# Seven block products in place of eight for the output GEMM of four token blocks

## The chip, the cores and the metric

The kernel runs on one core of a Trainium2 chip. The metric is the device time of one execution in microseconds; before the change it is 1434.03 us, the median of three runs (1433.68 to 1438.57). The core's engines run their own instruction lists in order: TensorE (PE, with its weight loads as PEld), the vector engine (DVE), ScalarE (ACT), GpSimd (POOL), and SyncE (SP), which issues the DMAs.

## The reference

An attention step is followed by two gated MLPs ("MoE" in the names), all in float32:

```
scores = x @ state.T / 8 ; a = softmax ; xread = a @ state          # per batch and head
a2 = softmax(state @ x.T / 8) ; sread = a2 @ x
x  = concat(xread, sread)                    # 8 batches x (512 + 32) tokens, 512 wide
x  = ((x @ w_a) * (x @ w_b)) @ w_out         # first MoE, d_ff = 1536
out = (silu(x @ w_gate) * (x @ w_val)) @ w_out2   # second MoE, d_ff = 1536
```

The 8 batches are 8 blocks of 512 tokens; the 8 x 32 state tokens are one block of 256 more, the "s block".

## The kernel before

**Precision.** A float32 operand is kept as two parts, a high part that the matmul's fp32r format holds exactly and the remainder as a low part. A product takes three matmuls: high x high, high x low, low x high. Splitting is one cast on ACT and one subtraction on DVE (`hi_lo`, `split`). A *pass* here is one matmul of a 128 x 128 stationary tile with 512 moving columns. The weights come as 64-bit numbers and are converted on ACT, DVE and GpSimd (`convert`).

**First MoE.** d_ff is cut into 12 steps f of 128 columns; two steps make a step pair fp. The gate and value GEMMs of a step (`gemm`, line 670) multiply the attention weights (two tiles of 128 x 512, high and low) with products of state and w_a, w_b (`sw`, lines 457, 458, 474), 6 passes each. The gate's bank `ab0` is copied to SBUF, the value's bank `ab1` is multiplied into it on DVE (`moe`, line 689), and the result `a` is split into `hs`. The output GEMM (`out_part`, line 705) adds 4 x 3 passes per step into the four banks `po0` to `po3`, two steps behind. Blocks 0 to 3 go together in pieces of four steps, since the state products are being made then; after that come blocks 4, 5, 6, the s block and block 7, one after the other. The output weights `wo1` stay in SBUF.

**Second MoE.** Blocks go in pairs (u, v). For the gate and value GEMMs (`product`, line 798) a 2 x 2 block product is done with 7 products instead of 8, on sums of blocks and weights; so is its output GEMM: 2 x 2 over (u, v) and (even step, odd step) against the output columns in halves. `operand_sums` makes the sums of the hidden values on DVE, `unit` (line 957) is one of the 7 products for half of the columns over a *chunk* of 3 step pairs, 9 passes, and adds and stores the partial results (`acc`). The 14 units of a chunk are dealt out between the GEMMs of the next chunk (`between`). The second MoE's weights are made by `second_weights` from block 4 on, sent to DRAM (`w2`, `wt`) and loaded when wanted.

**Attention.** `attention` loads x, transposed, in four tiles, makes both score matrices and both softmaxes. For blocks 0 and 1 the scores by rows (`pr`, line 519) are matmuls of their own, 32 columns wide; for the others the transposed scores (`psc`, line 530) are turned on DVE.

**Order.** No engine's order is written by hand. `Program.order` simulates the engines with a cost per operation, and takes, of the tasks whose inputs are there, the one with the earliest due time `by`; the order in which it starts them is the instruction order. Tasks with `start` (loads, some splits) wait for the planner's clock, which TensorE's main work drives. `FIRST_US`, `STRETCH`, `LEAD`, `ATT`, `DUE`, `AHEAD_US` set due times and starts, `ROOM` and `RESERVE` the tiles in SBUF (42 "w" tiles of 4 KB per partition, 26 "h" tiles of 2 KB). Forty-four spare pairs of matmuls on an identity (`warm`, line 1069) fill places where TensorE would have nothing.

## Time and profile before

| | |
|---|---|
| median of 3 runs | 1434.03 us |
| the profiled execution's own time | 1437.74 us |
| its span, first to last instruction | 1436.0 us |
| busy: PE / PEld / DVE / ACT / POOL | 1427.4 / 1181.3 / 1010.6 / 712.3 / 105.2 us |
| mean granted TensorE clock | 0.995 of 2.4 GHz |
| DMA, all queues | 344.26 MB, 240 GB/s, 67.7% of 16 engines |

The busy time of an engine is the time in which it has at least one instruction running. Matmuls overlap: one lasts some 390 ns, and the next starts some 226 ns after it. So the price of a matmul is read from the distance of starts, or from how many fit in a stretch, and not from its duration. The same holds, less so, for DVE and ACT.

### The profile page before, as it was taken

Reading aid. Unit: us, or ns where it says so; the run is one execution under the profiler, and the core shown is the slowest. Engines: PE = TensorE matmul, PEld = TensorE weight load, DVE = VectorE, ACT = ScalarE, POOL = GpSimd, SP = SyncE. Lnnn points to the kernel's source line nnn. Section 1 sums busy time; section 2 is a strip of 40 time slices with the busy share of each in tenths; the row PEclk is TensorE's granted clock in tenths of the full one; section 3 lists DMA queues with packets and bytes.
Section 4 is the critical chain, followed back from the end, with each engine's and each line's share of the span. In section 5 each row is a group of like instructions: output and inputs, shape, how many; then the busy total and the mean of one; then the engine's idle time right before and its main releaser. Section 6 shows DMA issues by size and latency. Waiting matters only on the chain.

```text
span 1436.0 us, 20514 instructions
## 1 busy us (share of the span) xinstructions
PE 1427.4 (99%) x7344; PEld 1181.3 (82%) x7344; DVE 1010.6 (70%) x1722; ACT 712.3 (50%) x1264; POOL 105.2 (7%) x78
## 2 busy tenths in 40 slices
PE   9999999999999999999999999999999999999998
PEld 7777788778787878998888888888888888888887
DVE  6799857875778787875796895556855477554454
ACT  6677756753556566644654453335333353323340
POOL 3102201100011101111010000000000000000000
PEclk9999999999999999999999999999999999999999
DMA  8874853943456757856988795766947578376476
GB/s 292 277 255 166 282 201 126 313 166 113 154 215 247 260 209 261 309 201 220 380 317 289 266 381 205 261 227 213 371 149 263 183 278 294 132 251 223 144 260 237
DMA packets 134424, 344.26 MB, mean 240 GB/s; under 512 B 14001, under 2 KB 16049, under 8 KB 134321
## 3 DMA queue, kind: packets, MB, share of 16 engines
q1 hardware_dynamic: 134320, 342.94, 67.7%
q8 instruction: 58, 0.95, 0.3%
q14 instruction: 46, 0.37, 0.1%
HBM read 246.42 MB, written 95.94 MB: 238 GB/s over the span
## 4 chain that ended last, share of the span: by engine, by line
PE 95%; DVE 2%; ACT 1%; DMA 1%; SPq 0%; issue 0%; ACTq 0%; DVEq 0%
PE pX L798 18%; PE p L670 17%; PE po L705 17%; PE pu L957 16%; PE pC L798 9%; PE pY L798 5%; PE p_s L670 2%; PE po_s L705 1%; PE pvs L670 1%; PE pgs L670 1%; PE sw L457 1%; PE pus L1012 1%; PE sw L458 1%; DMA xt<-in_xt 1%; PE psc L530 1%; PE pr L519 1%
## 5 line engine op out<-in xcount | busy, mean ns | idle before, releaser
L705 PE MATMUL po<-hs,wo 128*128 128x512 f32 x1152 | 283.3, 391 | 0.1
L705 PEld LDWEIGHTS po<-hs,wo 128*128 128x128 f32 x1152 | 214.7, 188 | 47.1 <-issue 1.6
L957 PE MATMUL pu<-S,wt 128*128 128x512 f32 x1008 | 242.7, 389 | 0.0
L670 PE MATMUL p<-xs,swh 128*128 128x512 f32 x768 | 239.6, 393 | 0.0
L957 PEld LDWEIGHTS pu<-S,wt 128*128 128x128 f32 x1008 | 188.9, 188 | 39.0
L798 PE MATMUL pX<-x,w 128*128 128x512 f32 x864 | 219.4, 389 | 0.0
L798 PEld LDWEIGHTS pX<-x,w 128*128 128x128 f32 x864 | 161.9, 188 | 33.7 <-ACT t L334 0.3
L670 PEld LDWEIGHTS p<-xs,swh 128*128 128x128 f32 x768 | 143.2, 189 | 35.0 <-issue 2.4
L670 PE MATMUL p<-xs,swl 128*128 128x512 f32 x384 | 150.1, 391 | 0.0
L806 DVE TENSOR_TENSOR t<-t,pC 128x512 f32<-128x512 f32 x96 | 65.9, 687 | 106.3 <-ACT t L334 94.1
L689 DVE TENSOR_TENSOR a<-a,p 128x512 f32<-128x512 f32 x96 | 65.7, 685 | 79.3 <-PE p L670 69.7
L334 ACT COPY a<-p 128x512 f32<-128x512 f32 x82 | 48.2, 587 | 100.3 <-PE p L670 99.8
L334 ACT COPY t<-pX 128x512 f32<-128x512 f32 x83 | 48.8, 588 | 98.6 <-PE pX L798 97.2
L349 ACT CAST hs<-a 128x512 fp32r<-128x512 f32 x96 | 59.7, 622 | 57.5 <-DVE a L689 44.4
L670 PEld LDWEIGHTS p<-xs,swl 128*128 128x128 f32 x384 | 72.4, 188 | 15.4
L798 PE MATMUL pX<-x,wg 128*128 128x512 f32 x288 | 73.2, 390 | 0.0
L798 PE MATMUL pY<-x,wg 128*128 128x512 f32 x288 | 73.1, 389 | 0.0
L342 DVE TENSOR_TENSOR hs<-a,hs 128x512 fp32r<-128x512 f32 x96 | 67.3, 703 | 8.3 <-ACT hs L349 7.5
L798 PE MATMUL pC<-x,w 128*128 128x512 f32 x288 | 73.1, 389 | 0.0
L798 PE MATMUL pC<-x,wv 128*128 128x512 f32 x288 | 73.1, 389 | 0.0
L342 DVE TENSOR_TENSOR swl<-swr,swh 128x1024 fp32r<-128x1024 f32 x48 | 60.6, 1262 | 11.0 <-PE p L670 4.7
L812 ACT ACTIVATE gv<-pX 128x512 f32<-128x512 f32 x48 | 28.7, 598 | 74.1 <-PE pX L798 74.1
(183 smaller groups left out, 2165.3 us busy)
## 6 DMA issues: line engine op xcount, KB each, us to landing
w<-w SPq DMA_DIRECT2D x120, 512.0 KB, 5.8
wt<-wt SPq DMA_DIRECT2D x84, 512.0 KB, 6.6
sw<-swo SPq DMA_DIRECT2D x96, 256.0 KB, 3.1
wg<-w2g SPq DMA_DIRECT2D x48, 512.0 KB, 5.6
swr<-sw SPq DMA_DIRECT2D x47, 512.0 KB, 5.2
raw_w<-in_wab SPq DMA_DIRECT2D x24, 512.0 KB, 5.6
wv<-w2v SPq DMA_DIRECT2D x36, 256.0 KB, 6.5
xt<-in_xt SPq DMA_DIRECT2D x32, 256.0 KB, 5.5
```

Of the source, the lines that this page charges most:

```text
L334: self.nc.scalar.copy(out(), in_())
L342: lambda e: self.by_engine[e].tensor_tensor(out=out(), in0=in0(), in1=in1(), op=ALU.subtract), r, w, **kw
L349: self.p.add(act(n), lambda e: self.nc.scalar.copy(hi(), src()), [src_buf], [hb], **kw)
L457: pe.matmul(ps.t, lhsT=hi.t[:, c], rhs=w.t[:, h], start=True, stop=False)
L458: pe.matmul(ps.t, lhsT=lo.t[:, c], rhs=w.t[:, h], start=False, stop=True)
L670: pe.matmul(ps.t[:, :n], lhsT=l, rhs=r, start=i == 0, stop=i == last)
L689: self.vec(n, lambda v, a=a, pb=pb: v.tensor_tensor(out=a.t[:, :n], in0=a.t[:, :n], in1=pb.t[:, :n], op=ALU.mult), [pb], [a])
L705: pe.matmul(ps.t[:, :n], lhsT=wo[f].t[:, hw, c], rhs=hs.t[:, hh, :n], start=st, stop=sp)
L798: pe.matmul(ps.t, lhsT=w.t[:, half, hw, i * P:(i + 1) * P], rhs=x.t[:, hx], start=start and i == n == 0, stop=stop and i == 1 and n == 2, ...
L806: self.vec(512, lambda e: e.tensor_tensor(out=to(), in0=a(), in1=b(), op=op), r, [w], **kw)
L812: self.p.add(act(n), lambda e: self.nc.scalar.activation(out=out.t[:, :n], in_=ps.t[:, :n], func=AF.Silu), [ps], [out])
L957: pe.matmul(ps.t, lhsT=w.t[:, half, hw, c], rhs=x.t[:, hx], start=starts and k == m == 0, stop=stops and k == n - 1 and m == 2, skip_group ...
```

## The change

1. **Output GEMM of blocks 4 to 7 as block products.** Blocks 4 and 5, then 6 and 7 run through a new `pair`: the gate and value GEMMs of both blocks for two steps, then `operand_sums`, and after three step pairs (`CHUNK_1`) the 14 units of a chunk, dealt out between the following GEMMs. The combined output weights are made by `first_combined` during blocks 0 to 3 and stand in DRAM (`wt1`).
2. **The s block goes last**, and takes in the units that pair (6, 7) leaves. Its output weights are loaded from `wt1` (`out_s_part`).
3. **Scores by rows of blocks 0 and 1** are now the transposed scores turned by TensorE (`turned`, four 128 x 128 transposes for each half).
4. **The second MoE's weights of steps 7 to 11** (`DIRECT`) are kept in SBUF from their making until pair (0, 1) uses them; the other pairs load them as before. The conversion starts at a fixed planned time (`FROM_US`) and its pace is bent (`PACE`).
5. **The planner's numbers** are others.

The core of the diff:

```diff
-FIRST_US = 30.0
-STRETCH = (1.302, 1.605)
+FIRST_US = 27.597
+STRETCH = (1.302, 1.8)
...
+CHUNK_1 = 3
+STAGGER = 40
+FROM_US = 230
+DIRECT = 7
...
-AHEAD_US = {"t": 16.0, "s": 10.0, "acc": 8.0, "w": 24.0, "x": 16.0}
+AHEAD_US = {"t": 19.412, "s": 10.168, "acc": 6.583, "w": 12, "x": 40}
...
-            self.pe(3.6 + SWITCH_US, by_rows, [raw_st, *xt], pr, by=start + span * 0.15)
...
-            out.append(self.softmax1(b, h, pr[h] if pr else sT, by_x))
+            out.append(self.softmax1(b, h, self.turned(b, h, sT, due + 3) if b < BY_ROWS else sT, by_x))
...
+    def turned(self, b, h, sT, by):
+        ps = self.ring(f"ab{h}", 1, f"pr{b}_{h}", self.ps) if b == 0 else self.bank(f"pr{b}_{h}")
+
+        def turn(pe):
+            for c in range(4):
+                r = slice(c * P, (c + 1) * P)
+                pe.transpose(ps.t[:, r], sT.t[:, r], self.ident.t)
...
+    def pair(self, u, v, xs, ws, chunk):
+        rhs = {b: lambda b=b: [(x.t[:, 0], x.t[:, 1]) for x in xs[b]] for b in (u, v)}
+        for lo in range(0, NFP, chunk):
+            made = {q: [] for q in range(1, 8)}
+            waiting, due = len(self.units), 0
+
+            def between():
+                nonlocal due
+                if self.pending:
+                    return self.pending.pop(0)()
+                due += waiting
+                while due >= 8 * chunk:
+                    due -= 8 * chunk
+                    self.unit()
+
+            for fp in range(lo, lo + chunk):
...
+                for b in (u, v):
+                    for o in range(2):
...
+                        self.gemm(pa, T, lhs[0], rhs[b], bufs[0], xs[b])
+                        a = self.h_buf(f"a{nm}")
+                        self.copy(lambda a=a: a.t, lambda pa=pa: pa.t, T, [pa], [a])
+                        between()
+                        pb = self.ring("ab1", 1, f"p{nm}_1", self.ps)
+                        self.gemm(pb, T, lhs[1], rhs[b], bufs[1], xs[b])
+                        self.plus(None, at, lambda a=a: a.t, lambda pb=pb: pb.t, [a, pb], to, ALU.mult)
+                        between()
+                self.operand_sums(f"1_{u}_{fp}", U, ve, V, made)
+            while self.units:
+                self.unit()
+            ck = dict(u=u, v=v, lo=lo, n=chunk, made=made, last=lo + chunk == NFP, step=1)
+            self.units = [(ck, q, i) for q in (1, 2, 6, 5, 7, 4, 3) for i in range(2)]
...
+    def first_combined(self, fp, wo, start):
...
+        c3, c4 = self.combined(f"f{fp}", *raw)
+        for k, c, at in (("3", c3, slice(2, 4)), ("4", c4, slice(4, 6))):
+            self.kept(f"wt1{k}{fp}", c, lambda c=c: c.t, d, lambda x, at=at: x[:, at], lambda t: t)
...
-                w = {k: self.loaded(f, k, f"w{k}{nm}", t0) for k in "g21"}
+                w = {k: self.loaded(f, k, f"w{k}{nm}", t0) for k in "g21" if u or f < DIRECT}
...
+                if f >= DIRECT and u == 0:
+                    w = {k: self.made2[f, k] for k in "g21v"}
...
-        order = TOGETHER + [(b, 0, NF) for b in [*range(4, 7), "s", 7]]
+        order = TOGETHER + [((4, 5), 0, NF), ((6, 7), 0, NF), ("s", 0, NF)]
```

How this moves the instructions is shown at three places.

TensorE, between the first and the second GEMM of block 0: `p_0_0_0` and `p_0_0_1` are the banks of block 0's gate and value GEMM, `pr` the scores by rows of block 1, `psc` its transposed scores, `xt` its x tiles. Before:

```order
L670 MATMUL p_0_0_0_367<-xs_1_313,swl_0_354 128x512
L519 MATMUL pr_0_379<-strt_99,xt_0_320 128x32
L519 MATMUL pr_1_380<-strt_99,xt_0_320 128x32
L519 MATMUL pr_0_379<-strt_99,xt_1_326 128x32
L519 MATMUL pr_1_380<-strt_99,xt_1_326 128x32
```

After:

```order
L523 MATMUL psc_0_357<-xt_3_321,strt_99 32x512
L523 MATMUL psc_1_358<-xt_3_321,strt_99 32x512
L674 MATMUL p_0_0_1_371<-xs_0_302,swh_0_319 128x512 x2
L674 MATMUL p_0_0_1_371<-xs_0_302,swl_0_333 128x512
L674 MATMUL p_0_0_1_371<-xs_1_310,swh_0_319 128x512 x2
L674 MATMUL p_0_0_1_371<-xs_1_310,swl_0_333 128x512
L541 MATMUL pr_0_390<-ident,sT_0_379 128x128 x4
L541 MATMUL pr_1_398<-ident,sT_1_381 128x128 x4
```

Before, the first four of 32 narrow matmuls are shown (28 more follow, and then `p_0_0_1`); after, the 8 wide matmuls of `psc` end ahead of `p_0_0_1`, and 8 transposes stand behind it.

TensorE in block 4, from step 8 on before and from step 6 on after: `p_4_8_1` is the value GEMM of block 4's step 8, `po` an output bank, `pu` the bank of a unit with `S` the sums of hidden values and `wt` the combined weights. Before:

```order
L670 MATMUL p_4_8_1_4205<-xs_0_3278,swh_4_4117 128x512 x2
L670 MATMUL p_4_8_1_4205<-xs_0_3278,swl_4_4142 128x512
L670 MATMUL p_4_8_1_4205<-xs_1_3281,swh_4_4117 128x512 x2
L670 MATMUL p_4_8_1_4205<-xs_1_3281,swl_4_4142 128x512
L705 MATMUL po_4_0_3869<-hs_4_6_4137,wo_6_1986 128x512 x3
L705 MATMUL po_4_1_3915<-hs_4_6_4137,wo_6_1986 128x512 x3
L705 MATMUL po_4_2_3923<-hs_4_6_4137,wo_6_1986 128x512 x3
L705 MATMUL po_4_3_3931<-hs_4_6_4137,wo_6_1986 128x512 x3
L670 MATMUL p_4_9_0_4237<-xs_0_3278,swh_4_4117 128x512 x2
```

After:

```order
L674 MATMUL p_4_6_1_4576<-xs_1_3190,swl_3_4374 128x512
L674 MATMUL p_4_7_0_4587<-xs_0_3168,swh_3_4358 128x512 x2
L674 MATMUL p_4_7_0_4587<-xs_0_3168,swl_3_4374 128x512
L674 MATMUL p_4_7_0_4587<-xs_1_3190,swh_3_4358 128x512 x2
L674 MATMUL p_4_7_0_4587<-xs_1_3190,swl_3_4374 128x512
L1079 MATMUL pu_4_0_1_1_4599<-S_4_0_1_0_4440,wt_4_0_1_0_4287 128x512 x3
L1079 MATMUL pu_4_0_1_1_4599<-S_4_0_1_1_4444,wt_4_0_1_1_4303 128x512 x3
L1079 MATMUL pu_4_0_1_1_4599<-S_4_0_1_2_4447,wt_4_0_1_2_4319 128x512 x3
L674 MATMUL p_4_7_1_4625<-xs_0_3168,swh_3_4358 128x512 x2
```

Twelve output passes stood behind every value GEMM; now a unit of 9 passes stands behind about every second GEMM, and in the first chunk of pair (4, 5), where no units wait yet, none.

The vector engine beside it: `a` and `hs` are the gated product and its low part, `U`, `V` and `ve` products of the pair's hidden values, `S` their sums and the low parts of these, `swl` the low part of a gate weight, `cv`, `c` and `w` the second MoE's weights. Before:

```order
L689 TENSOR_TENSOR a_4_8_4212<-a_4_8_4212,p_4_8_1_4205 128x512
L342 TENSOR_TENSOR swl_5_4228<-swr_5_4179,swh_5_4217 128x1024
L342 TENSOR_TENSOR hs_4_8_4223<-a_4_8_4212,hs_4_8_4223 128x512
L388 TENSOR_SCALAR cv_v_4230<-cv_v_4230 128x512
L393 TENSOR_SCALAR cv_v_4230<-cv_v_4230 128x512
L396 SCALAR_TENSOR_TENSOR cv_v_4230<-raw_v_4200,cv_v_4230 128x512
L689 TENSOR_TENSOR a_4_9_4254<-a_4_9_4254,p_4_9_1_4246 128x512
```

After:

```order
L921 TENSOR_TENSOR S_1_4_1_4425<-ve_4_1_4360,V_4_1_4386 128x512
L837 TENSOR_TENSOR c_1_4429<-cv_o_4266 128x256
L921 TENSOR_TENSOR U_4_2_4442<-a_4_4_4422,p_4_4_1_4415 128x512
L348 TENSOR_TENSOR S_4_0_1_0_4440<-U_4_0_4043,S_4_0_1_0_4440 128x512
L348 TENSOR_TENSOR S_4_0_1_1_4444<-U_4_1_4264,S_4_0_1_1_4444 128x512
L348 TENSOR_TENSOR S_4_0_1_2_4447<-U_4_2_4442,S_4_0_1_2_4447 128x512
L921 TENSOR_TENSOR S_1_4_1_4425<-S_1_4_1_4425,U_4_1_4264 128x512
L921 TENSOR_TENSOR U_4_2_4442<-a_4_5_4459,p_4_5_1_4449 128x512
```

Between two products that read a value bank (`U_4_2` from `p_4_4_1` and from `p_4_5_1`) stand four sums and splits of other steps.

## Rows read from the trace of the kernel before

**Rows 1.** The page: busy us (share of the span) xinstructions, by engine

```profile
PE 1427.4 (99%) x7344; PEld 1181.3 (82%) x7344; DVE 1010.6 (70%) x1722; ACT 712.3 (50%) x1264; POOL 105.2 (7%) x78
```

**Rows 2.** The page: the chain that ended last, shares by engine

```profile
PE 95%; DVE 2%; ACT 1%; DMA 1%; SPq 0%; issue 0%; ACTq 0%; DVEq 0%
```

**Rows 3.** Waits of PE: who waited for whom, us in total, times, longest

```profile
PE pr L519 <- DMA xt<-in_xt: 1.6, 4, 0.8
PE sw L457 <- ACT swo L334: 1.4, 5, 0.5
```

**Rows 4.** Windows: stretch, length, busy (xcount) per engine, PEclk, DMA share, GB/s

```profile
100.00:200.00 100.00, 99.46 (x622) 79.57 (x622) 82.68 (x155) 70.03 (x131) 18.41 (x12) 1.00 0.63 216
700.00:800.00 100.00, 100.00 (x443) 82.83 (x442) 76.69 (x133) 50.82 (x89) 9.66 (x7) 1.00 0.86 309
```

**Rows 5.** Groups by form on PE: xcount, busy us, mean ns, idle before

```profile
L705 PE MATMUL po<-hs,wo 128*128 128x512 f32 x1152 | 283.3, 391 | 0.1
...
L519 PE MATMUL pr<-strt,xt 64*128 64x32 f32 x128 | 10.8, 319 | 1.7 <-DMA xt<-in_xt 1.6
```

**Rows 6.** The chain of waits up to 60 us: start us, us, what

```profile
9.22 3.52 PE pr L519 x52
...
28.43 6.28 DMA xt<-in_xt
34.75 5.01 PE pr L519 x52
...
50.10 0.87 PE pat L583 x8
```

**Rows 7.** Timeline of PE: start us, us, engine, line, op, tiles, xcount

```profile
50.81 2.84 PE L1069 MATMUL warm<-ident 128*128 128x128 f32 x24
...
54.64 0.73 PE L670 MATMUL p<-xs,swh 128*128 128x512 f32 x2
...
65.17 1.09 PE L530 MATMUL psc<-xt,strt 64*32 64x512 f32 x16
```

**Rows 8.** Windows: the second gate GEMM, block 5, a dense stretch, the fullest DMA

```profile
39.69:43.81 4.12, 4.12 (x14) 3.30 (x13) 3.59 (x6) 2.18 (x4) 0.00 (x0) 0.67 1.04 398
432.00:501.00 69.00, 69.00 (x379) 56.10 (x378) 56.12 (x102) 41.13 (x71) 8.23 (x7) 1.00 0.71 251
443.00:470.00 27.00, 27.00 (x195) 21.26 (x194) 25.51 (x46) 17.73 (x33) 2.68 (x3) 1.00 0.56 202
682.00:718.00 36.00, 36.00 (x161) 29.81 (x160) 27.54 (x45) 21.83 (x38) 1.29 (x1) 1.00 1.00 380
```

**Rows 9.** Timeline of DVE in block 5, where instructions stand back to back

```profile
449.05 1.22 DVE L342 TENSOR_TENSOR swl<-swr,swh 128x1024 fp32r<-128x1024 f32 x1
450.19 0.68 DVE L559 TENSOR_TENSOR sn<-sn,mx 128x512 f32<-128x512 f32 x1
450.79 0.69 DVE L342 TENSOR_TENSOR hs<-a,hs 128x512 fp32r<-128x512 f32 x1
...
464.03 0.41 DVE L725 TENSOR_TENSOR c<-cv_v 128x256 f32<-128x256 f32 x1
464.36 0.41 DVE L725 TENSOR_TENSOR c<-cv_v,c 128x256 f32<-128x256 f32 x1
```

**Rows 10.** Timeline of all engines in block 5: last gate matmul, output passes, product

```profile
440.38 0.39 PE L670 MATMUL p<-xs,swl 128*128 128x512 f32 x1
...
440.60 1.75 PE L705 MATMUL po<-hs,wo 128*128 128x512 f32 x7
440.87 0.69 DVE L689 TENSOR_TENSOR a<-a,p 128x512 f32<-128x512 f32 x1 [0.93 <-PE p L670]
```

**Rows 11.** Timeline of all engines at the start: DVE beside GpSimd

```profile
7.46 0.42 DVE L388 TENSOR_SCALAR cv_w<-cv_w 128x512 f32<-128x512 f32 x1
7.70 1.30 POOL L400 TENSOR_TENSOR cv_w<-cv_w 128x512 int32<-128x512 int32 x1 [6.39 <-DVE cv_w L396]
...
7.91 1.37 DVE L393 TENSOR_SCALAR cv_w<-cv_w 128x512 uint32<-128x512 uint32 x1
```

More of the change, by code (lines that the diff above doesn't have):

```diff
@@ L509, in attention @@
         ]
[L510 to L525 removed]
+        due = start + span * 0.15
         psc = [self.bank(f"psc{b}_{h}", h if b == 0 else None) for h in range(2)]
@@ L673, in gemm, with weights, of @@
         self.main(3 * len(xs) * (PASS_US if n == 512 else HALF_PASS_US), fn, [*bufs, *xs], [ps])
+    def weights(self, get, pairs):
+        def of(f):
+            t = get(f)
+            cs = [slice((f % 2) * 256 + ab * P, (f % 2) * 256 + ab * P + P) for ab in range(2)]
+            return [lambda c=c: pairs(t, c) for c in cs], [t, t]
+        return of
     def moe(self, blk, n, xs, ws, wo, steps=(0, NF)):
@@ L711, in moe, with out_s_part, fn @@
             self.pending.append(out_part)
-    def second_weights(self, f, start, gap):
+    def out_s_part(self, f, hs, po):
+        wt = self.wt1[f // 2]
+        w = self.w_buf(f"wo1s{f}", shape=(2, 2, 256))
+        self.dma(
+            lambda: w.t.bitcast(F32), lambda: wt.t[:, slice(0, 8, 7) if f % 2 == 0 else slice(1, 7, 5)], [wt], [w],
+            P * 4096, start=self.clock - AHEAD_US["t"] * self.stretch
+        )
+        if f == 0:
+            po.extend(self.bank(f"po0_s_{k}") for k in range(2))
+        for j in range(KD):
+            ps, c, k = po[j // 2], slice(j % 2 * ST, j % 2 * ST + ST), j // 2
+            def fn(pe, ps=ps, c=c, k=k, j=j):
+                lc = slice(j % 2 * P, j % 2 * P + P)
+                for i, (hh, hw) in enumerate(((0, 0), (1, 0), (0, 1))):
+                    pe.matmul(
+                        ps.t[:, c], lhsT=w.t[:, k, hw, lc], rhs=hs.t[:, hh, :ST], start=f == i == j % 2 == 0,
+                        stop=f == NF - 1 and i == 2, skip_group_check=True
+                    )
+            self.main(3 * HALF_PASS_US, fn, [hs, w], [ps])
+        if f < NF - 1:
+            return
+        by, d = self.clock + 3, self.x2["s"]
+        for j in range(KD):
+            o, ps, c = self.h_buf(f"o0_s_{j}"), po[j // 2], slice(j % 2 * ST, j % 2 * ST + ST)
+            self.copy(lambda o=o: o.t[:, :ST], lambda ps=ps, c=c: ps.t[:, c], ST, [ps], [o], by=by)
+            self.dma(lambda j=j: d.t[j], lambda o=o: o.t[:, :ST], [o], [(d, j)], P * 1024, by=by + 3)
@@ L860, in second @@
                 self.silu(gv, X)
-                self.product(3, C, ops, w["v"], 1 if xs_s else 0, False, True)
+                self.product(3, C, ops, w["v"], whole, False, True)
                 self.add(t2, t2, C)
@@ L874, in second @@
                 self.unit()
-            ck = dict(u=u, v=v, lo=lo, n=chunk, made=made, last=last)
+            ck = dict(u=u, v=v, lo=lo, n=chunk, made=made, last=last, step=2)
             self.units = [(ck, q, i) for q in (1, 2, 6, 5, 7, 4, 3) for i in range(2)]
@@ L926, in unit @@
         u, v, lo, n = ck["u"], ck["v"], ck["lo"], ck["n"]
-        nm = f"{u}_{lo}_{q}"
+        nm = f"{ck['step']}_{u}_{lo}_{q}"
+        wt = self.wt1 if ck["step"] == 1 else self.wt
+        ahead = lambda k: self.clock - AHEAD_US[k] * self.stretch
         if i == 0:
@@ L934, in unit @@
                     b = self.h_buf(f"wt{nm}_{fp}", R32, (1, 2, 256)) if one else self.w_buf(f"wt{nm}_{fp}", shape=(2, 2, 256))
-                    d = self.wt[fp]
+                    d = wt[fp]
                     self.dma(
                         lambda b=b: b.t.bitcast(F32), lambda d=d, k=2 if not one else 1: d.t[:, at:at + k], [d], [b],
-                        P * (2048 if one else 4096), start=self.clock - AHEAD_US["t"]
+                        P * (2048 if one else 4096), start=ahead("t")
                     )
@@ L941, in unit @@
             ck["s"] = [
-                self.split(f"S{nm}_{k}", buf, of, start=self.clock - AHEAD_US["s"])
+                self.split(f"S{nm}_{k}", buf, of, start=ahead("s"))
                 for k, (buf, of) in enumerate(ck["made"][q])
@@ L947, in unit @@
             tag = f"X{i}" if q == 1 else f"Y{i}"
-            ck[tag] = self.ring(f"po{2 + i}", 1, f"pu{nm}_{i}", self.ps) if q == 1 else self.bank(f"pu{nm}_{i}")
+            po = 2 + i if q == 1 else i if ck["step"] == 1 else None
+            ck[tag] = self.bank(f"pu{nm}_{i}", po)
         ps = ck[f"X{i}" if q in (1, 6, 7, 4) else f"Y{i}"]
```

216 lines of the change are left out of this document (135 added, 81 removed).

## The prediction

> **What bounds the kernel now.** I read the page first, then the waits of TensorE, then the stretches. TensorE is busy for 99% of the span, with the vector engine next at 70% [rows 1]; matmuls are pipelined, so that share alone proves little. The chain that ended last is 95% TensorE [rows 2], and TensorE's whole idle time with a named cause is a few microseconds: 1.6 for x tiles of block 1's scores, 1.4 for state products [rows 3]. So the reader is to see an engine that is fed without a gap, and the price of a main pass is the pace of a full stretch: 443 matmuls in 100 us, 225.7 ns each [rows 4]. Whatever leaves TensorE's list shortens the run, if what feeds TensorE still keeps up. Both halves have to be worked out.
>
> **What the change takes off TensorE.** Term 1. The output GEMM of blocks 4 to 7 loses 4 x 12 x 12 = 576 of the 1152 passes in the first row of [rows 5]; two pairs, two chunks each, 14 block products of 9 passes add 504. The gate and value passes (4 x 12 x 12) and the s block's 256-column passes stay the same in number. Net 72 passes x 225.7 ns = 16.3 us, all on the path.
>
> Term 2 is the scores of blocks 0 and 1. The 128 narrow matmuls of the second row of [rows 5], 10.8 us, go; 16 transposes come, at the price of block 1's present ones, 8 in 0.87 us, so 1.7 us [rows 6]. This is not a plain subtraction, because the stretch waits for block 1's attention. There the last x tile lands at 28.43 + 6.28 = 34.71, the narrow matmuls run until 39.76, the transposes of the result come at 50.10 and block 1's first GEMM at 54.64 [rows 6, 7]; ahead of it TensorE runs 24 fillers on an identity [rows 7], so it has nothing else to do. After: scores (16 passes, 1.09 us [rows 7]), one gate GEMM of block 0 (6 passes, 1.35 us) that covers the copy of the scores, then the transposes, 0.87: free at about 38.0 and not 39.76, 1.8 us sooner with the same landing. The landing can come sooner too: block 0's own narrow matmuls, 3.52 us of them in one run on the chain at 9.22 [rows 6], no longer stand ahead of its state products, and the loads of block 1's x are issued two places earlier on SP. A third piece is the clock: from 39.69 to 43.81, straight after the narrow matmuls, the granted clock averages 0.67 [rows 8], that is partly at 1.2 GHz and not 2.4; its 12 passes cost 4.12 us where 12 x 225.7 ns is 2.7, and 1.4 us come back if the clock stays up. Bounds: nothing, if softmax and weight conversion on the vector engine are the later input anyway; 10.8 - 1.7 + 1.4 = 10.5 us, if all of it reaches the path. I take 5, the middle, since the chain argument gives 1.8 + 1.4 and the sooner landing is worth a little more.
>
> **What it adds elsewhere.** The operand sums and the high and low parts of S fall to the vector engine. Per pair of blocks and pair of steps it has had 4 gate products and 4 low parts, 8 instructions; it now has 4 products, 5 sums and 7 low parts, 16. Six such groups in two pairs add 96; the sums of partial results add 20 per pair, 40; the combined weights add 24 subtractions (256 wide) and 12 low parts. At a start-to-start pace of 0.60 us for 512 columns and 0.33 for 256 [rows 9] that is 148 x 0.60 + 24 x 0.33 = 97 us of vector work. In the stage that matters, from the first product of block 4 to the first of the s block, the order of the changed kernel has 388 vector instructions: 281 at 0.60, 58 at 0.33, 22 of 1024 columns at 1.14, 27 tiny ones at about 0.1, together 215 us. TensorE has 576 gate and 378 product passes there, 24 of block 3, and two blocks' attention; one block with its attention takes 69.0 us against 288 x 0.2257 = 65.0, so 4.0 each [rows 8]. Together 229 us. The vector engine is then at 0.94 of TensorE's time; before it was 56.1 of 69 [rows 8], 0.81. The second MoE's weight conversions start earlier and run longer, which is why the share is not still higher.
>
> Term 3 is what this closeness costs. In the second GEMM of a step, the product must have read the bank before the next one writes it. At present 12 output passes and a GEMM lie between: the last matmul starts at 440.38, output passes start at 440.60, the product runs from 440.87 to 441.56 [rows 10]. In the first chunk of pair (4, 5) only one GEMM lies between, 1.35 us: the next use could start at 441.95, and the product ends at 441.56 if the vector engine is free. About 0.2 to 0.4 us is left after the signal. It isn't free when a 1.14 us split stands in front. Some 11 such places (at a few, pieces of block 5's attention lie between too), none to 1.14 us each: 0 to 12.5. I take 3, since in a stretch as dense as the new one (25.5 of 27 us from 443) TensorE lost nothing [rows 8]. A gain here is excluded, since TensorE has no wait in this stage to lose. Later chunks have 9 product passes between as well and stand as they did.
>
> Of the rest I cost at nothing: the combined weights of blocks 4 to 7, made during blocks 0 to 3 beside their GEMMs (24 x 0.33 + 12 x 0.60 = 15 us of vector work and 12 casts; if late, the first products wait); the s block's output weights, now 12 loads and not held tiles, fetched ahead in the s block; the 20 weight tiles of the second MoE kept in SBUF, which spare 20 loads but hold 20 of 42 tiles until pair (0, 1) uses them (if room runs short, loads start late).
>
> Sum against the profiled execution's own 1437.74 us: - 16.3 - 5 + 3 gives 1419.4. That execution stands 3.7 above the median of the runs, 1434.03; so 1415.7, say **1416 us**.
>
> **A lock between two engines.** From 7.91 a shift on the vector engine takes 1.37 us, where the clamp of the same width just before took 0.42, and GpSimd's addition runs from 7.70 to 9.00 beside it [rows 11]: 0.95 us lost. The order has 13 such additions in the stage. If each costs 0.95, the vector engine loses 12 us, and its 0.94 becomes 0.99, without any room; put wholly on the path that is 1428. If the two seldom meet, the sum stays as it is. I keep the sum, and count the lock in the first rival's chance. The Trainium skill, page SBUF — State Buffer, section "Who interferes with whom", says that these two engines share one pair of ports as an exclusive lock and that the second to come is blocked for the whole instruction. The trace agrees, with the 0.95 us above.
>
> **Rivals.** First, the vector engine becomes the bound of blocks 4 to 7. For it: 0.94 of TensorE's time on instructions that wait for TensorE, ScalarE and DMAs in a fixed order, where no 100 us of this profile has it above 82.7 busy [rows 4]. If 0.827 is what it can sustain, 215 us of work take 260 and TensorE loses 31: 1434.0 - 16.3 - 5 + 31 = 1444, slower than before. It decides from 21.3 us of waits on. Against it: the dense 27 us of [rows 8].
>
> Second, the DMA queue. By the sizes in the order the changed kernel moves 389 MB and not 343. Between the first weights of block 4 and the first x of the second MoE it issues 96 MB where it was 75, in about 290 us (229, some 50 of the s block, 126 x 0.2257 = 28 of the products in it, less 20 as the x is loaded ahead): 330 GB/s. In the fullest stretch of the profile 380 GB/s were moved at a share of 1.00, with TensorE at 36 of 36 us [rows 8]; over a longer one 309 [rows 4]. At 309 the 96 MB take 311 us, 21 too long, and the run ends at 1434.0 - 18.3 + 21 = 1437, the same as before. Against it: the product weights, the largest part of it, are asked for 19.4 x 1.8 = 35 planned us ahead, and an x tile lands in 6.28 [rows 6]. More likely a few tiles are late in bursts, say 10 us in all: 1426.
>
> Third, all of the early scores reach the path and nothing waits: 1434.0 - 16.3 - 10.5 = 1407.
>
> **How the numbers follow.** A measurement of this kernel tells no change from a change of about 0.5%, 7.2 us: faster is below 1426.9, slower above 1441.2. The forecast, TensorE's list with small waits, 1410 to 1423: 0.56. The third rival, 1405 to 1410: 0.12. Late tiles, 1423 to 1437: 0.18, of which 0.10 is still below 1426.9. The vector engine as the bound, 1430 to 1450: 0.14, half of it above 1441.2, 0.06 within. This gives faster 0.79, same 0.14, slower 0.07. The range that leaves out two in ten: from 1406 to 1429; the forecast's own is 1410 to 1423.
>
> **What would show it.** Right: TensorE's busy time down by about 26 us with the share still at 98% or more; 576 output passes and 1512 product passes at 226 ns apart; block 1's first GEMM at 48 to 52 us; no fall of the granted clock after 35; waits on the vector engine's products in blocks 4 and 5 of 3 us in all. Wrong: TensorE waiting for DVE on p banks, or for DVE or DMA ahead of products, by over 10 us between 345 and 575; DMA at a share of 1.0 for long there with TensorE waiting for wt or S tiles; new waits at the start of the second MoE.

## The result, and the profile after

The changed kernel takes 1419.93 us (median of 4 runs, 1418.21 to 1421.42); the kernel before, run beside it again, takes 1436.15 (4 runs, 1433.68 to 1438.57). The ratio is 0.9887 [0.9862, 0.9912]: 16 us faster, where 1416 were forecast with a range of 1406 to 1429. The profiled execution took 1420.18 us of its own time; the forecast in the same terms was 1419.4.

The page of the changed kernel, the lines that answer to [rows 1, 2]:

```profile
PE 1403.9 (99%) x7160; PEld 1159.2 (82%) x7160; DVE 1107.4 (78%) x1887; ACT 730.2 (51%) x1307; POOL 105.8 (7%) x78
...
PE 88%; DVE 6%; DMA 2%; issue 2%; ACT 1%; SPq 0%; POOL 0%; ACTq 0%; DVEq 0%; POOLq 0%
```

TensorE's busy time fell by 23.5 us, and the share stayed at 99%. VectorE has 97 us more, as the prediction counted. It now makes 6% of the chain that ended last, where it had 2%: there are places again where TensorE waits for it.

The groups by form on TensorE (xcount, busy us, mean ns, idle before) answer to [rows 5]:

```profile
L1079 PE MATMUL pu<-S,wt 128*128 128x512 f32 x1512 | 366.4, 390 | 0.0
...
L725 PE MATMUL po<-hs,wo 128*128 128x512 f32 x576 | 143.2, 391 | 0.0
```

The counts are those of the prediction. Where the time went is read best from the places of the program on the time axis. The table has the starts of some first matmuls, in us, read from the profiled execution of each kernel; the experiments below are in it too. "Stage" is the time from block 4's first GEMM to the second MoE (blocks 4 to 7 and the s block), "pairs 0-3" that of the second MoE's first four blocks, "gaps" what TensorE lost in them beyond its pace (distances between starts of more than 0.3 us, less the usual 0.227).

| kernel | block 1 | block 4 | second MoE | last matmul | stage | pairs 0-3 | gaps |
|---|---|---|---|---|---|---|---|
| before | 54.6 | 363.6 | 695.1 | 1431.8 | 331.5 | 322.3 | 0.0 |
| after | 47.8 | 356.8 | 673.8 | 1414.1 | 317.0 | 325.8 | 3.2 |
| e_turned_only | 48.6 | 358.9 | 690.4 | 1426.9 | 331.5 | 322.3 | 0.0 |
| e_rows_again | 52.8 | 365.3 | 679.4 | 1433.6 | 314.1 | 340.0 | 17.5 |
| e_rows_fixed | 67.5 | 379.3 | 697.5 | 1436.8 | 318.2 | 325.2 | 2.7 |
| e_eighth | 48.0 | 356.4 | 688.0 | 1427.7 | 331.6 | 325.6 | 3.1 |
| e_sums_24 | 46.2 | 354.5 | 683.5 | 1422.1 | 329.0 | 324.5 | 1.9 |
| e_sums_72 | 48.0 | 356.3 | 724.4 | 1464.1 | 368.1 | 325.6 | 3.0 |
| e_dve_24 | 46.6 | 354.1 | 671.2 | 1429.4 | 317.1 | 344.1 | 21.5 |
| e_dve_72 | 46.2 | 355.1 | 676.6 | 1434.3 | 321.5 | 343.5 | 20.9 |
| e_no_handover | 46.4 | 354.6 | 672.7 | 1415.9 | 318.1 | 329.1 | 6.6 |
| e_conv_early | 47.2 | 355.4 | 669.9 | 1415.0 | 314.5 | 330.9 | 8.3 |
| e_small_pool | 46.4 | 354.3 | 670.6 | 1408.3 | 316.3 | 323.6 | 1.1 |
| e_light_conv | 46.4 | 355.2 | 672.4 | 1411.4 | 317.2 | 324.9 | 2.3 |

Kernels with one order of instructions differ by up to 2.5 us in where block 4 starts (354.3 to 356.8), so that column tells nothing below that; the stage, counted from there, is steadier.

From before to after: 6.8 us sooner at block 1, and the same at block 4; 14.5 us less in the stage; 3.5 us more in the second MoE's first four blocks; nothing in the rest. Together 17.8, and the last matmul starts 17.7 us sooner.

Two of these figures hold more than they show, because 32 score matmuls (`psc`, two blocks' worth) now run ahead of block 1. Sixteen of them have left the stage. Their windows before and after (stretch, length, busy and xcount of PE, PEclk, DMA share, GB/s):

```profile
363.60:695.10 331.50, 3.27 (x48) 1.00 0.66 234
356.80:673.80 317.00, 2.18 (x32) 1.00 0.87 310
```

All other counts of TensorE in the stage differ by the 72 passes alone. e_rows_again has the counts of the changed kernel there and no idle time at all (stretch, length, busy and xcount of PE, PEld, DVE, ACT, POOL, then PEclk, DMA share, GB/s):

```profile
365.30:679.40 314.10, 314.10 (x1861) 266.29 (x1860) 299.56 (x524) 188.51 (x341) 31.39 (x19) 1.00 0.86 301
```

So some 17.4 us of work have left the stage (16.3 of passes, about 1.1 of scores), and about 2.8 us of waits have come into it. Blocks 1 to 3, from block 1 to block 4, take 309.0 us in both kernels; here they are before, after, and in e_turned_only:

```profile
54.60:363.60 309.00, 307.34 (x1638) 245.06 (x1637) 240.78 (x410) 191.99 (x335) 41.53 (x27) 1.00 0.61 211
47.80:356.80 309.00, 304.41 (x1613) 244.10 (x1613) 282.54 (x492) 213.48 (x378) 44.92 (x31) 1.00 0.84 291
48.60:358.90 310.30, 306.00 (x1611) 245.00 (x1610) 245.20 (x413) 190.22 (x331) 40.54 (x27) 0.99 0.62 211
```

TensorE has less to do there after the change (16 score matmuls and 12 fillers fewer, 4 state products more), and idles 4.6 us where it idled 1.7. e_turned_only has no combined weights to make and idles 4.3, so they are not shown to be the cause.

The start of the changed kernel, timeline of TensorE (start us, us, engine, line, op, tiles, xcount, idle before), beside [rows 6, 7]:

```profile
29.59 2.16 PE L523 MATMUL psc<-xt,strt 64*32 64x512 f32 x16
...
33.17 1.04 PE L541 MATMUL pr<-ident,sT 128*128 128x128 f32 x8
...
47.76 0.73 PE L674 MATMUL p<-xs,swh 128*128 128x512 f32 x2
```

The turned scores of block 1 are done at 34.2, where the prediction had 38.0, since block 1's x has landed already. Windows of the stretch up to block 1, of the stage and two parts of it, and two that answer to [rows 4], in the same form:

```profile
35.00:48.00 13.00, 12.08 (x82) 8.40 (x81) 11.58 (x22) 11.11 (x20) 2.56 (x2) 1.00 0.98 359
100.00:200.00 100.00, 97.76 (x616) 78.89 (x615) 86.64 (x151) 69.12 (x129) 20.25 (x14) 1.00 0.75 258
357.00:674.00 317.00, 315.45 (x1863) 266.19 (x1862) 302.53 (x538) 193.67 (x351) 34.45 (x22) 1.00 0.87 310
400.00:464.00 64.00, 64.00 (x294) 52.05 (x294) 62.89 (x109) 38.25 (x65) 2.59 (x2) 1.00 0.65 221
592.00:674.00 82.00, 81.92 (x564) 76.18 (x563) 79.35 (x148) 50.59 (x101) 8.58 (x6) 1.00 1.01 363
700.00:800.00 100.00, 98.85 (x435) 81.00 (x434) 77.56 (x128) 48.74 (x86) 7.65 (x6) 1.00 0.80 286
```

The granted clock no longer falls after 35. In blocks 4 and 5 VectorE is busy 62.9 of 64 us, and TensorE loses nothing; in the s block the DMA stands at a share of 1.01 for 82 us, and TensorE loses 0.1. New are the losses in the two stretches of [rows 4]: 97.8 us busy from 100 to 200 where it had 99.5, and 435 matmuls from 700 to 800 where it had 443.

Waits of TensorE from 674 to 1000 (engine, line, tile, whom it waited for, us, times, longest):

```profile
PE pX L913 <- DVE c L342: 0.9, 1, 0.9
PE pX L913 <- DVE t L342: 0.7, 1, 0.7
PE pX L913 <- ACT t L340: 0.3, 1, 0.3
PE pX L913 <- DMA w<-w: 0.3, 1, 0.3
```

The longest of them, in the timeline of GpSimd, VectorE and TensorE:

```profile
774.53 1.29 POOL L406 TENSOR_TENSOR cv_g<-cv_g 128x512 int32<-128x512 int32 x1 [4.55 <-DMA wt<-wt]
774.79 2.18 DVE L348 TENSOR_TENSOR w<-c,w 128x512 fp32r<-128x512 f32 x2
776.89 0.68 DVE L348 TENSOR_TENSOR w2g<-cv_g,w2g 128x512 fp32r<-128x512 f32 x1
777.49 0.68 DVE L342 COPY c<-pX 128x512 f32<-128x512 f32 x1
778.23 0.96 PE L913 MATMUL pX<-x,w 128*128 128x512 f32 x3 [0.89 <-DVE c L342]
```

Two subtractions on VectorE take 2.18 us beside GpSimd's addition (1.29 in e_small_pool, where the addition is cut), as in [rows 11]. The copy that empties TensorE's X bank stands behind them, so TensorE waits.

### The profile page after: what moved, and what is told of

The parts are those of the page before. It is cut to its first block, busy times and chain, and to the rows that moved or that the text cites. A ratio compares the mean times of both kernels' runs of the same rounds, so it can differ in the third digit from the quotient of the medians.

```text
span 1418.1 us, 20685 instructions
## 1 busy us (share of the span) xinstructions
PE 1403.9 (99%) x7160; PEld 1159.2 (82%) x7160; DVE 1107.4 (78%) x1887; ACT 730.2 (51%) x1307; POOL 105.8 (7%) x78
## 4 chain that ended last, share of the span: by engine, by line
PE 88%; DVE 6%; DMA 2%; issue 2%; ACT 1%; SPq 0%; POOL 0%; ACTq 0%; DVEq 0%; POOLq 0%
PE pu L1079 23%; PE pX L913 17%; PE p L674 16%; PE pC L913 9%; PE po L725 7%; PE pY L913 4%; PE p_s L674 2%; PE warm L1194 1%; PE sw L465 1%; PE po_s L750 1%; PE pvs L674 1%; PE pgs L674 1%; PE pus L1137 1%; PE sw L466 1%; DVE w L348 1%
## 5 line engine op out<-in xcount | busy, mean ns | idle before, releaser
L1079 PE MATMUL pu<-S,wt 128*128 128x512 f32 x1512 | 366.4, 390 | 0.0
L1079 PEld LDWEIGHTS pu<-S,wt 128*128 128x128 f32 x1512 | 282.4, 188 | 58.9 <-issue 0.8
L725 PE MATMUL po<-hs,wo 128*128 128x512 f32 x576 | 143.2, 391 | 0.0
L725 PEld LDWEIGHTS po<-hs,wo 128*128 128x128 f32 x576 | 107.5, 188 | 24.9 <-issue 2.4
L348 DVE TENSOR_TENSOR S<-S,S 128x512 fp32r<-128x512 f32 x108 | 70.9, 696 | 6.6 <-ACT S L355 5.4
L355 ACT CAST S<-S 128x512 fp32r<-128x512 f32 x108 | 61.6, 620 | 20.6 <-PE pX L913 9.8
L913 PE MATMUL pX<-x,wg 128*128 128x512 f32 x258 | 65.7, 390 | 0.0
L913 PE MATMUL pY<-x,wg 128*128 128x512 f32 x258 | 65.5, 389 | 0.0
L913 PE MATMUL pC<-x,wv 128*128 128x512 f32 x258 | 65.5, 389 | 0.0
L355 ACT CAST swh<-swr 128x1024 fp32r<-128x1024 f32 x48 | 50.6, 1054 | 26.9 <-DMA swr<-sw 21.5
```

The lines of the kernel that those rows point to most:

```text
L348: lambda e: self.by_engine[e].tensor_tensor(out=out(), in0=in0(), in1=in1(), op=ALU.subtract), r, w, **kw
L355: self.p.add(act(n), lambda e: self.nc.scalar.copy(hi(), src()), [src_buf], [hb], **kw)
L725: pe.matmul(ps.t[:, :n], lhsT=wo[f].t[:, hw, c], rhs=hs.t[:, hh, :n], start=st, stop=sp)
L913: pe.matmul(ps.t, lhsT=w.t[:, half, hw, i * P:(i + 1) * P], rhs=x.t[:, hx], start=start and i == n == 0, stop=stop and i == 1 and n == 2, ...
L1079: pe.matmul(ps.t, lhsT=w.t[:, half, hw, c], rhs=x.t[:, hx], start=starts and k == m == 0, stop=stops and k == n - 1 and m == 2, skip_group ...
```

## The experiments

The questions were: are TensorE's passes worth their pace (term 1); did the scores give the gain at the start (term 2); how near is VectorE to setting the pace in blocks 4 to 7 (term 3 and the first rival); and what took 3.5 us in the second MoE. Unless said otherwise, "against after" is the difference of medians to 1419.93; each ratio is to the kernel before, run on the same chip.

**The passes alone.** Order of every engine held; the product q = 1 is run twice into one bank:

```diff
+        twice = 2 if q == 1 and ck["step"] == 1 else 1
         def fn(pe):
-            for k, (w, x) in enumerate(zip(ws, ss)):
+            for _ in range(twice):
+                for k, (w, x) in enumerate(zip(ws, ss)):
...
```

> The changed kernel, but the first of the 7 products of each chunk of blocks 4 to 7 is run twice into the same bank, the second time starting the sum anew, so the result is that of the changed kernel: 72 passes of 128x512 more, which is the number that the change took away. No other engine gets work. Theory (TensorE alone is the bound in this stage): 72 x 225.7 ns = +16.3 us, to 1436. Rival (VectorE, 95 to 98% busy there, already sets part of the pace, so that more TensorE time is partly hidden): +5 to +12 us, to 1425 to 1432, and the waits of that stage shrink.

1432.09 us (1429.92 to 1433.57, 12 runs), ratio 0.9975 [0.9966, 0.9984]; 12.2 above after. The stage takes 331.6 us, 14.6 more than after for 72 x 225.7 ns = 16.25 of passes. So 1.7 us of them vanished. Waits of TensorE there, first of the changed kernel:

```profile
PE pst L655 <- ACT sr L650: 0.8, 1, 0.8
PE p L674 <- DVE U L921: 0.7, 1, 0.7
```

and with the product repeated:

```profile
PE pst L655 <- ACT sr L650: 0.8, 1, 0.8
```

The wait for VectorE's product is gone. In the stage, then, the theory holds for nine tenths, and the rest is what the rival says: a little of VectorE's pace shows in the changed kernel, 1.7 us of it. The whole time leans further to the rival: 12.2 us in the medians, 13.6 at the last matmul of the traces, where small differences ahead of block 4 and behind the stage come in.

**The scores alone, from both sides.** First the kernel before with the turned scores only (the diff's new function, and its call in place of the 64 matmuls):

> The kernel before with one part of the change alone: the scores of blocks 0 and 1 are transposed on TensorE from the scores that exist by columns, instead of being computed a second time by rows. The hand-written start times stay those of before. Theory (the scores themselves stood on the path): block 1's first GEMM moves from 54.6 us to 47 to 50, the granted clock does not fall between 35 and 60 us, and the time falls by 5 to 7 us, to about 1430. Rival (the 6.8 us that the changed kernel gained ahead of block 1 came from its new table of start times, not from the scores): block 1's first GEMM stays at 53 to 55 us and the time at 1435 to 1437.

1431.98 us (1430.24 to 1433.89, 12 runs), ratio 0.9979 [0.9969, 0.9988]: 3.0 us faster, 1.7 to 4.4. In the traces block 1 starts 6.0 us sooner and the last matmul 4.9. The rival is out; the size is somewhat under the theory's, and the clock does fall, if later: windows of this kernel,

```profile
35.00:48.00 13.00, 10.27 (x69) 7.66 (x67) 10.40 (x19) 11.60 (x20) 3.16 (x2) 1.00 0.77 279
48.00:60.00 12.00, 11.98 (x45) 9.44 (x47) 11.31 (x18) 6.54 (x12) 1.35 (x1) 0.86 0.90 299
```

After 10.27 busy us in 13, part of the next 12 us is at 1.2 GHz. The changed kernel has more matmuls ahead of block 1 (82 and not 69 in these 13 us), and there the clock stays up; that the one is the cause of the other was not tried. Then the changed kernel with scores by rows again:

```diff
+            self.pe(3.6 + SWITCH_US, by_rows, [raw_st, *xt], pr, by=start + span * 0.15)
...
-            out.append(self.softmax1(b, h, self.turned(b, h, sT, due + 3) if b < BY_ROWS else sT, by_x))
+            out.append(self.softmax1(b, h, pr[h] if pr else sT, by_x))
```

> The changed kernel with the scores of blocks 0 and 1 computed by rows again for their softmax (64 small matmuls a block, as before), in place of the four transposes for each group; the scores by columns stay at their new, early place and every start time stays. Theory (scores on the path): block 1's first GEMM goes back from 47.8 us to 53 to 55, and the time rises by 5 to 8 us, to 1425 to 1428. Rival (start times did it): block 1 at 48 to 50 us, time 1420 to 1422.

1439.38 us (5 runs, 1438.08 to 1440.31), ratio 1.0032 [1.0020, 1.0044]: 19.5 above after, far over both. Block 1 starts at 52.8, 5.0 later than after, and the second MoE 5.6 later: so far the theory. The other 14 us arise in the second MoE's first four blocks, 340.0 us with waits such as

```profile
PE pu L1083 <- DVE S L348: 6.0, 1, 6.0
PE pu L1083 <- DMA wt<-wt: 4.8, 2, 4.2
```

Nothing was edited there. But the planner orders all that follows from its modelled times, and some 9 us of work at the start (10.8 of narrow matmuls for 1.7 of transposes) gave another order 700 us later. So the whole time of such a run does not price the edit. The same with the order held, the by-row matmuls put into the place of the transposes:

```diff
-            for c in range(4):
-                r = slice(c * P, (c + 1) * P)
-                pe.transpose(ps.t[:, r], sT.t[:, r], self.ident.t)
+            for c in range(4):
+                for h, j, rows, cs in heads:
+                    if h == g:
+                        pe.matmul(ps.t[...], lhsT=xt[j].t[rows, c * P:(c + 1) * P], rhs=raw_st.t[rows, cs], ...)
```

> The changed kernel with the scores of blocks 0 and 1 computed by rows again, in the place of the four transposes of each group and with every other engine's order held. (Where the planner was told of it, the second MoE's first pair was ordered anew and lost 14 us of its own, so that the whole time said nothing.) Theory (these matmuls stand on the path before block 1's first GEMM): block 1 at 52 to 55 us instead of 47.8, time +5 to +8 us against the changed kernel, 1425 to 1428. Rival (the start times made the gain): block 1 at 48 to 50 us, time 1420 to 1422.

1441.86 us (8 runs, 1439.34 to 1446.97), ratio 1.0048 [1.0030, 1.0066]; block 1 starts 19.7 us later than in after, and all of it stays to the end (22.7 at the last matmul). The rival is out, but the size is not the one expected, because this edit changed more than was meant: all 32 matmuls of a group lie on one half of the rows, so that a block's 64 run as 32 on one half and then 32 on the other. Timeline of TensorE and windows of this kernel:

```profile
11.80 9.43 PE L542 MATMUL pr<-strt,xt 64*128 64x32 f32 x64
21.16 2.93 PE L1198 MATMUL warm<-ident 128*128 128x128 f32 x12
```

```profile
12.00:21.00 9.00, 9.00 (x64) 9.00 (x63) 2.90 (x6) 2.96 (x5) 2.80 (x2) 0.71 0.77 306
21.00:24.00 3.00, 3.00 (x14) 2.73 (x13) 1.89 (x3) 0.00 (x0) 0.00 (x0) 0.50 0.00 0
```

They start 112 ns apart at full clock. In the kernel before, which alternates the halves, the second of a pair starts 6 or 7 ns after the first and the next pair 105 ns later: half the price. So e_rows_fixed is an upper bound, and e_rows_again (+5.0 at block 1) and e_turned_only (-6.0) give the price, 5 to 6 us at block 1, though each with an order planned anew.

**VectorE's room, with the planner told.** More sums behind the operand sums of blocks 4 to 7, each a repeat with the same result:

```diff
+        if nm.startswith("1_"):
+            for i in range(2):
+                if i % 3 == 0:
+                    plus(5, lambda: ve.t, t(4), [ve, buf(4)], ALU.add)
...
```

> The changed kernel with 24 more VectorE sums of 0.6 us each (two repeated for each pair of gate tiles of blocks 4 to 7, with the same result): +14.4 us of VectorE work in a stage of 235 us that has 223 us of it. Asked: how near VectorE is to setting the pace there. Theory A (VectorE's spare time is usable, only the excess shows): 237.6 of work in 235, +2 to +5 us. Theory B (its order leaves nothing usable, each sum shows): +14 us. Theory C (conversions that are not due yet move out of the stage): 0 to +1 us, with VectorE busier in the second MoE.

> The changed kernel with 72 such sums more in blocks 4 to 7 (the same result): +43 us of VectorE work, 266 us in a stage of 235. Theory A: +31 us or somewhat more, to 1451 to 1456, the stage at 98% of VectorE. Theory B: +43 us, 1463. Theory C: +10 to +20 us, as the conversions move out of the stage.

With 24: 1437.55 us (10 runs, 1435.30 to 1440.58), ratio 1.0017 [1.0005, 1.0028]. With 72 (six repeats and not two): 1441.14 (4 runs, 1440.08 to 1441.52), ratio 1.0046 [1.0030, 1.0063]. None of the three theories: 17.6 and 21.2 above after. The stage took 317.1 us with 24 more, the same as after, and 321.5 with 72; the second MoE's first four blocks took 18 us more in both. Theory C has the place right and the price wrong: conversions did move out of the stage (16 GpSimd additions in its 317 us where the changed kernel has 22), and the loss came there, in the second MoE. Windows of 780 to 840, of the changed kernel and of that with 24 sums:

```profile
780.00:840.00 60.00, 59.00 (x259) 48.17 (x258) 58.73 (x100) 32.65 (x60) 4.25 (x3) 1.00 0.89 315
```

```profile
780.00:840.00 60.00, 45.95 (x178) 35.51 (x178) 58.08 (x101) 34.87 (x62) 7.01 (x5) 0.91 0.80 292
```

VectorE is full in both (58 of 60 us): what is left of the conversions meets the operands of the next pair here. With a little more of it TensorE loses 14 of the 60 us, and the clock falls after its idle time, to 0.91 on the mean.

**VectorE's room, order held.** The same repeats in the place of the sum that they repeat, without the planner's knowledge:

```diff
+        times = {5: 1, 6: 1, 7: 2, 3: 2} if nm.startswith("1_") else {5: 1, 6: 1, 7: 1, 3: 1}
+        def plus(q, a, b, r, op):
+            def fn(e):
+                for _ in range(times[q]):
+                    e.tensor_tensor(out=t(q)(), in0=a(), in1=b(), op=op)
...
```

> The 24 further VectorE sums in blocks 4 to 7 again, but with every engine's order held as in the changed kernel: the repeats stand right behind the sum that they repeat, and the planner does not count them. (With the planner counting them the stage lost nothing, and the second MoE's first pair lost 18 us: its instructions had been ordered anew.) Theory A (VectorE's spare time in the stage is usable): 0 to +5 us against the changed kernel, 1420 to 1425. Theory B (each sum shows): +14 us, 1434.

> The same with 72 further sums, +43 us of VectorE work, order held. Theory A: VectorE has 223 us of work in 235, so some 12 us of it are free: about +31 us, 1451, TensorE waiting for VectorE all through blocks 4 to 7. Theory B: +43 us, 1463. Theory C (work of the stage is so loosely due that it runs late without being missed): under +15 us.

With 24: 1427.88 us (4 runs, 1426.99 to 1428.54), ratio 0.9951 [0.9934, 0.9968]; the stage 329.0 us, 12.0 more for 14.4 of sums. With 72: 1468.35 (4 runs, 1465.67 to 1472.88), ratio 1.0237 [1.0210, 1.0263]; the stage 368.1, 51.1 more for 43.2. In the stage that is theory B, nearly: each us of VectorE's work shows. In the whole time 24 sums cost 8.0 us, between the two theories: that run reaches block 4 2.3 us sooner, as others with this order do, and loses 1.3 us less in the second MoE, for a reason given below. Windows of the stage with 24, then with 72 sums:

```profile
355.00:684.00 329.00, 319.63 (x1862) 266.93 (x1861) 318.27 (x563) 194.16 (x352) 33.79 (x22) 0.99 0.84 298
```

```profile
357.00:724.00 367.00, 330.48 (x1855) 271.35 (x1854) 352.22 (x610) 192.92 (x349) 34.35 (x22) 0.97 0.76 267
```

and TensorE's largest waits with 72:

```profile
PE p L674 <- DVE U L921: 18.0, 9, 4.6
PE p L674 <- DVE V L921: 8.2, 6, 2.5
PE p L674 <- DVE ve L921: 5.6, 3, 3.0
```

These are the p banks that the prediction named, waiting for VectorE's products. All named waits of this stretch add up to 36 us; the clock at 0.97 over 367 us is at most another 11. In the changed kernel VectorE is idle for 14.5 of the stage's 317 us, which would have held the 24 sums, but those holes lie where it waits for others, and not where the sums stand.

**What the second MoE's first pairs lost.** Four runs. Without the hand-over in SBUF (`DIRECT = 7` to `12`):

> The changed kernel without the hand-over in SBUF: the weights of all 12 feature blocks of the second MoE's first pair go through DRAM, as before the change. Asked: where the 3.6 us come from that the second MoE's pair (0,1) lost in the changed kernel. Theory A (the conversions of the second MoE's weights, whose GpSimd step shares a port with VectorE, now stand where TensorE waits for VectorE to empty its X banks): pair (0,1) still shows gaps of about 1 us at GpSimd steps, in all 3 to 5 us of waits; time 1419 to 1422. Theory B (the held tiles shorten the pool of weight tiles, which delays the loads of that pair): the waits fall to 1 us or less and the time to 1416 to 1417.

1421.80 us (4 runs, 1421.19 to 1422.25), ratio 0.9910 [0.9896, 0.9925]; the gaps grew from 3.2 to 6.6 us, 3.5 of it one wait:

```profile
PE pu L1079 <- DMA wt<-wt: 3.5, 1, 3.5
```

The changed kernel's waits in these blocks are all gone, and this one has come, behind which TensorE runs for a while at 1.2 GHz; the window of it (form as above):

```profile
820.00:827.00 7.00, 6.24 (x16) 4.89 (x17) 5.26 (x9) 4.78 (x10) 0.00 (x0) 0.53 1.04 407
```

Neither theory describes this. The planner saw this edit too and ordered anew, so the run does not price the held tiles; it shows that the kernel without them is no faster. Conversions due sooner (`NEXT_US = 154.749` to `110.0`):

> The changed kernel with one number changed: the conversions of the second MoE's weights are due by 110 us after the first MoE's end instead of 155. Theory A (conversions in pair (0,1) cause its 3.6 us): VectorE's and GpSimd's conversion work in that pair falls by about a third, the waits there by 1 to 2.5 us; but as much of that work moves into blocks 4 to 7, where VectorE is 95 to 98% busy: time 1417 to 1421. Theory B (hand-over): waits in pair (0,1) as in the changed kernel, time 1420 to 1422.

1420.39 us (4 runs, 1419.58 to 1420.86), ratio 0.9900 [0.9886, 0.9915]. The stage got 2.5 us shorter and the first four blocks 5.1 longer, with one wait of 3.2 us for the low part of an operand: neither theory. The edit didn't do what it was for: loads asked for sooner were ordered anew, and 11 of GpSimd's additions lie between 672 and 840 us where the changed kernel has 10. It decides nothing, but that this number alone brings no gain. GpSimd's additions cut, order held:

```diff
+        c = 16 if name[0] in "gvo" else 512
...
-            out=t.t[:, 0].bitcast(I32), in0=t.t[:, 0].bitcast(I32), in1=t.t[:, 1].bitcast(I32), op=ALU.add
+            out=t.t[:, 0, :c].bitcast(I32), in0=t.t[:, 0, :c].bitcast(I32), in1=t.t[:, 1, :c].bitcast(I32), op=ALU.add
```

> The changed kernel with the GpSimd step of the 36 conversions of the second MoE's weights cut from 512 columns to 16 (these weights come out wrong); all orders held. Asked: whether the port that GpSimd and VectorE share makes the 3.6 us lost in the second MoE's pair (0,1). Theory A (it does): the second MoE's first four blocks go from 325.8 us to 322 to 323, time 1416 to 1417. Theory B (VectorE is simply full there, 29.0 and 29.8 us of 30 between 780 and 840): 325 to 326 us, time 1419 to 1420.

1414.42 us (4 runs, 1413.34 to 1416.01), ratio 0.9858 [0.9841, 0.9876]. The first four blocks take 323.6 us and the gaps are 1.1 where they were 3.2; the two largest, 1.05 us at 778 and 0.91 at 811, are gone. The first of them stands in all five traces that have this order and no edit in the second MoE (after, e_eighth, e_sums_24, e_sums_72, e_rows_fixed). The second is missing in one of these, e_sums_24, and that run shows how it arises. GpSimd's addition and the sum on VectorE that falls beside it, of the changed kernel, then of e_sums_24:

```profile
804.54 1.29 POOL L406 TENSOR_TENSOR cv_o<-cv_o 128x512 int32<-128x512 int32 x1 [15.13 <-PE pC L913]
804.67 1.70 DVE L902 TENSOR_TENSOR s<-s,x2l 128x512 f32<-128x512 f32 x1 [0.35 <-DMA accc<-c]
```

```profile
814.22 0.69 DVE L902 TENSOR_TENSOR s<-s,x2l 128x512 f32<-128x512 f32 x1
814.33 1.74 POOL L406 TENSOR_TENSOR cv_o<-cv_o 128x512 int32<-128x512 int32 x1 [15.07 <-ACT x L355]
```

Where the addition starts first, the sum takes 1.0 us longer and the copy that TensorE waits for at 811 comes late; where the sum starts first, the addition takes longer and no wait of TensorE follows. So GpSimd's share is about two thirds of the loss, close to theory A. (Of the 5.5 us in the medians the trace puts 2.5 ahead of block 4, where other runs with this order start as soon; 0.7 lies in the stage.) And the last 9 conversions cut on VectorE as well, order held, the same slice on the clamp, the shift and the merge of the sign:

> The changed kernel with the VectorE and GpSimd steps of the last 9 conversions of the second MoE's weights (three of twelve feature blocks) cut from 512 columns to 16 (these weights come out wrong); all orders held. Takes about 13 us of VectorE work and 12 us of GpSimd work, nearly all out of the stretch from 690 to 840 us. Theory A or B of the run before (the conversions that are left over there cost the 3.6 us, by port or by VectorE's time): 321 to 323 us in the second MoE's first four blocks, time 1415 to 1417. Theory C (the operands of the next pair, sooner than before, cost it): 325 to 326 us, time 1419 to 1420.

1417.28 us (4 runs, 1417.05 to 1417.78), ratio 0.9878 [0.9859, 0.9898]. 324.9 us, gaps 2.3: less than the run before, though it takes out nearly the same GpSimd steps there and VectorE has 130 us of work from 672 to 840 and not 141. The gap at 778 is gone, but one of 0.73 us has come at another X bank, behind a copy on ScalarE. Its 2.3 lies within what runs with no edit there give (1.9 to 3.2), so this run adds little: less work on VectorE in all did not take the gaps away. The additions beside VectorE make the two largest gaps of the changed kernel; the rest is left open, as is the operands' part, which was not tried alone.

## Why the prediction was right

**Term 1, 16.3 us for 72 passes.** It stands. About 17.4 us of work left the stage, the passes and 1.1 us of scores that the prediction had left in place; e_eighth shows the same from the other side, 14.6 us in the stage for the same passes with 1.7 us of waits gone.

**Term 3, 3 us of waits.** The size came, 2.8 us, but not where it was reasoned to come. The first chunk of pair (4, 5), with its 11 close places, has no wait for a product. The two waits that show in the stage are 0.8 us in block 4 for ScalarE's `sr`, a part of the attention, and one in pair (6, 7), behind a unit, where the prediction had the later chunks "stand as they did":

```profile
473.32 0.74 PE L674 MATMUL p<-xs,swh 128*128 128x512 f32 x2 [0.68 <-DVE U L921]
```

So the mechanism, a bank that VectorE has not yet read, is real, but the agreement in size is partly luck. The density behind it was read well. From block 4 to the first product of the s block, in the form of the windows above:

```profile
356.80:592.00 235.20, 233.73 (x1301) 190.18 (x1301) 223.37 (x392) 143.27 (x252) 25.87 (x16) 1.00 0.82 292
```

VectorE's 223 us of 235 are 0.95, where 215 of 229 gave 0.94.

**Term 2, 5 us for the scores.** 6.8 us at block 1 in the traces, within the bounds of 0 and 10.5. The mechanism is shown by e_turned_only and e_rows_again. Of the clock's part, the fall at [rows 8]'s place is gone, but in e_turned_only another comes later, so the turned scores alone don't see to it. The scores were free sooner than the prediction dared to count, at 34.2 and not 38.0. What the new planner numbers give without the turned scores was not tried. (One reading in it is off without harm: of the 1.6 us of [rows 3], some 0.5 are waits of block 0's scores, and not of block 1's.)

**Costed at nothing.** The s block's loads cost nothing that shows: TensorE loses 0.1 us there. The combined weights are not shown to cost anything: TensorE idles 2.9 us more in blocks 1 to 3, but nearly as much in e_turned_only, which has none. The second MoE's start was not free: 3.5 us. The prediction listed new waits there among what would prove it wrong, but its reason, room for tiles, was not shown to be the cause; the two largest waits come from GpSimd's additions. The terms as they came out are - 16.3 - 6.8 - 1.1 + 2.8 + 3.5 = - 17.9, forecast - 18.3. So the sum is better than its parts: term 2's surplus of 1.8 and the moved scores' 1.1 happen to make up for most of the 3.5.

**The lock.** Kept out of the sum, rightly for blocks 4 to 7: with the additions all but gone, the stage is only 0.7 us shorter. It shows where VectorE's queue stands between TensorE and a bank, in the second MoE. The Trainium skill, page SBUF — State Buffer, section "Who interferes with whom", has the two engines exclude each other on a shared pair of ports; the trace agrees, with 2.18 us for two subtractions beside an addition.

**The first rival** did not come, but its mechanism is real and near. That 0.827 is all that VectorE can sustain is refuted by 62.9 of 64 us. Yet each further us of its work in that stage shows there by 0.8 or more, so the forecast held with next to no room: 14.4 us more took 12.0 in the stage, and 8.0 of the 16 from the whole time. **The second rival** is refuted: 363 GB/s at a share of 1.01 for 82 us, and TensorE fed. **The third**, 1407, is out by the 3.7 us of early scores that did not reach block 1, the stage's waits and the second MoE's.

## What to carry to other kernels

Where two engines are both nearly full in a stage (here TensorE and VectorE), price work on each by holding the order and repeating an instruction: in the stage 16 us of TensorE's passes showed 14.6, and 14.4 us of VectorE's sums showed 12.0, while 14.5 us of idle time stood in its row. Compare counts as well as times before calling a difference a wait: 16 matmuls had moved out of the stage unseen. In a kernel whose order is planned from modelled times, an edit that the planner sees is two edits: look at the stage that you changed, and at the first one behind it that shares its leftovers, before you believe the whole time. Deferred work is not free work: here the loss came where the next batch of inputs is made.
